# Routing 24 blocks in segments of 6, 6, 4, 4 and 4, and issuing joins and halvings behind copies out of the banks

## The chip, the core and the metric

The kernel runs on one core of one Trainium2 chip. A core has TensorE (PE, with its weight loads shown as PEld), VectorE (DVE), ScalarE (ACT), GpSimd (POOL) and SyncE (SP, which here only issues transfers). Each engine takes its own instructions in the order of the program and waits at one whose inputs or buffers are not ready. Matmul results land in PSUM, in eight banks; ACT and DVE copy them out. The metric is the device time of one execution in microseconds (us), the median of the runs.

## What is computed

A local and global attention, and on its output a mixture of eight experts of which each token takes two.

```python
def _attn_ref(q, k, v, n_global, n_local):      # 4 x 8 heads x 768 x 64; 8 global, 96 local
    ...
    scores = scale * np.matmul(q, k.transpose(0, 1, 3, 2)) + bias
    scores = np.where(keep, scores, -1000000000.0)
    a = np.exp(scores - scores.max(-1))
    return np.matmul(a / (a.sum(-1) + 1e-09), v)

def _moe_ref(x, w_gate, w_noise, noise, w1, w2):  # x 3072 x 512, 8 experts, hidden 1024
    noisy_logits = x @ w_gate + np.log1p(np.exp(x @ w_noise)) * noise
    top2 = np.argpartition(-noisy_logits, 2, axis=1)[:, :2]
    ...                                           # top2_w: softmax over the two
    for e in range(E):
        for k in range(2):
            mask = top2[:, k] == e
            h = np.maximum(x[mask] @ w1[e], 0.0)
            out[mask] += top2_w[mask, k, None] * (h @ w2[e])
```

## The kernel before

The 3072 tokens are 24 blocks of 128. The program writes its order out by hand: the order of calls in the source is the order of instructions on each engine.

**Attention.** A loop goes over half blocks (two of a block's four pairs of heads each). In each it computes scores, the exponential (ACT), transposes, the product with v, and the division (DVE, L910 to L915). Behind a finished block, `gate_t` transposes it (PE L380) and POOL splits its words into 16-bit halves (L236) for a store into `xd`; `gate_l` multiplies it with the gate weights (PE L410) and copies the result out (ACT L413); `gate_s` sums the partial results (PE L423 or L426). Blocks are taken in pairs within a segment: the second of a pair does the matmuls of both. A segment with an odd number of blocks leaves one block alone, which has its own matmuls.

**Routing.** The list `SEG` cuts the blocks into segments. `route(r)` is a generator: each `next` issues a few small instructions, mostly on DVE, that turn the gate results of segment r into the two chosen experts, weights and places. Its own PE work is a running count (L552, L554) and, in groups of up to three blocks, the entry into a table: masks (L579, on POOL for segments up to `CLOSE`, on DVE after), values (L603), six matmuls (L628), one addition (L632). In the attention loop `tick` and `finish` advance the generators of the segments in progress. What is left of the last two is advanced in `slots` between the matmuls of expert 0's first layer (`up(0, f)`, 32 slots of three matmuls). The first 512 tokens of expert 0 come from the segments up to `CLOSE`, so that expert 0 starts when the attention ends; their rows are stored once more, whole, in `xe`. When all segments are routed, `rank` sorts the other seven experts by load and their tokens are gathered.

**Experts.** Every factor is split into a high and a low part (`cut`: ACT rounds, L196; DVE subtracts, L197), and each product is three matmuls. Expert 0 works plainly. Experts 1 to 7 compute their first layer by seven products of half-size blocks (`first`, PE L1426) in four rounds c = 0 to 3; sums and copies out of the banks around them are ACT L1468, L1485, L1491 and L1113, and DVE L1462, L1478, L1500 and L1117. `between(c, slot)` issues what the table `ahead` lists: weights for a later round (`w[c][0..2]`, of which [1] waits for four sums on POOL, L1276 to L1279), halvings of the second layer's weights (`w2_`), gathers (`get`), DMA transposes (`tip`) and joins (`mix`). A join (`weave`, ACT L282 or DVE L284) puts the two 16-bit halves of a gathered, transposed tile together again. The second layer (`second`) is `down` (L1169) and `down_t` (L1192), into a ring of two banks; ACT copies each result of `down_t` out (L1201 for expert 0; L1198 and L1199 for the others), `back` transposes it (L1215), and `put` scales it (L1142) and adds it to the output by an indirect DMA (L1145). While `second(e)` runs, the list that `prepare(e + 1)` returns is worked off beside it: the next expert's tokens, `tokens(e, t)`, in the steps `one` (four sums, L1319 to L1322), `same`, `two` and `three` (halvings, each an ACT L196 and a DVE L197), with weights and joins between. In the traces the names are of the tiles: `aside` holds sums and the copies of `down_t`, `xg` a gathered tile, `xt` its 16-bit form, `wall` weights, `xh` and `xl` the high and the low part of tokens, `hh` and `hl` of the hidden layer.

Of the kernel before, what the change touches and what calls it, by code (L numbers as in the profile page):

```python
# [10 lines left out]
F32 = mybir.dt.float32  # L11
# [10 lines left out]
P = 128  # L22
# [13 lines left out]
def tile_local_global_attention_then_moe(  # L36
# [14 lines left out]
    B, _, _, D, _, HP, Q = q.shape  # L51
    H = 2 * HP
    Dm = H * D
# [3 lines left out]
    E, _, F = w1.shape  # L57
    KC, FC = Dm // P, F // P
    NG = kT.shape[2] // NB - P
    N = B * S  # L60
    NT = B * NB
# [1 line left out]
    windowed = 1 <= n_local <= NP + 1 and 0 <= n_global <= NG  # L63
    scale = 1.0 / math.sqrt(D)
    slopes = [2.0 ** (-8.0 * (h + 1) / H) for h in range(H)]
    SEG = [(0, 6), (6, 12), (12, 17), (17, 21), (21, NT)]
    CLOSE = 2
    SW = max(z - a for a, z in SEG)

# [5 lines left out]
    gp = wctx.enter_context(tc.tile_pool(name="gp", bufs=1))  # L75
# [13 lines left out]
    wd = dram.tile([N, E], F32, name="wd")  # L89
    xe = dram.tile([DUMP + SEG[CLOSE][1] * P, Dm], F32, name="xe")  # L90

# [118 lines left out]
    xg, xt, xw = {}, {}, {}  # L210
# [18 lines left out]
    def planes(x):  # L229
        return x.rearrange("p (h d) -> p h d", h=2)  # L230
# [7 lines left out]
    def gather(e, t, n=DUMP + N):  # L238
        if e >= E or t >= tiles(e):
            return  # L240
        if e == 0 and t < TA:
            n = DUMP + SEG[CLOSE][1] * P
            xw[e, t] = gp.tile([P, Dm], F32, name="xg", bufs=7)
# [115 lines left out]
    XR, XT, LS, stored, rowed = {}, {}, {}, {}, {}  # L359
# [5 lines left out]

    ALONE = [z - 1 for a, z in SEG if (z - a) % 2]

    def partner(g):
        if not windowed or g in ALONE:
            return None  # L370
        a = [a for a, z in SEG if a <= g < z][0]
        return (g - a) % 2

    def gate_t(g):
        x = rowed[g] = XR.pop(g).rearrange("p h d -> p (h d)")
        stored[g] = gp.tile([P, 2 * Dm], U16, name="xt", bufs=4)
        halved(planes(stored[g]), words(x))
        ps = bank("m").rearrange("p (k t) -> p k t", k=KC)
        for k in range(KC):
            nc.tensor.transpose(ps[:, k], x[:, k * P:(k + 1) * P], ident)  # L380
        j = partner(g)
        if j is None:
            XT[g] = ys[2].rearrange("p (k t) -> p k t", k=KC)
            to = XT[g]
        else:
            if j == 0:
                XT[g + 1] = pairs[0].rearrange("p (k j t) -> p k j t", k=KC, j=2)
            to = XT[g + 1 - j][:, :, j]
        nc.scalar.activation(to, ps, AF.Copy)

    def store(g):
# [2 lines left out]
    def gate_l(g, later=None):  # L394
        if g < SEG[CLOSE][1]:
            nc.sync.dma_start(xe[DUMP + g * P:DUMP + (g + 1) * P], rowed.pop(g))
        if later is None:
            store(g)
        else:
            later(store, g)  # L400
        j = partner(g)
        if j == 0:
            return
        ps = bank("m")[:, :P]
        x = XT.pop(g)
        x = [x] if j is None else [x[:, :, i] for i in range(2)]
        for i, y in enumerate(x):
            c = 2 * E * (1 - i)
            for k in range(KC):
                nc.tensor.matmul(ps[32 * k:32 * k + 32], wgn[:, c + 4 * E * k:][:, :4 * E], y[:, k], start=i == 0,  # L410
                                 stop=i + 1 == len(x), tile_position=(0, 32 * k))
        LS[g] = small.tile([P, P], F32, name="ls")
        nc.scalar.activation(LS[g], ps, AF.Copy)  # L413
# [15 lines left out]
    pairs = []  # L429
# [223 lines left out]
    with ExitStack() as actx:  # L653
# [34 lines left out]
        if windowed:  # L688
# [36 lines left out]
            t = small.tile([P, 1], F32, name="warm")  # L725
# [66 lines left out]
        routes, active = {}, []  # L792
# [3 lines left out]

        END, WAIT = 7, 8

        def begin():
            for x, _ in active:  # L800
                x.ready = {WAIT: 4, WAIT + 1: 6}.get(x.ready, 0)

        def go(y):
            x = y[0]
            v = next(x, 0)
            if v == 0:
                active.remove(y)
            elif v is True:
                x.ready = WAIT
            elif v == 2:  # L810
                x.ready = END
            elif v == LAST:
                x.ready = WAIT + 1

        def tick(place):
            for y in sorted(active, key=lambda y: y[1] != CLOSE):
                if y[0].ready <= place:
                    return go(y)

        def finish():  # L820
            for y in active[:]:
                n = 5 if y[1] >= CLOSE else 3
                while n and y in active and y[0].ready <= END:
                    go(y)
                    n -= 1

# [92 lines left out]
        todo = {}  # L919
# [85 lines left out]
        else:  # L1005
# [6 lines left out]
            for g in range(NT):  # L1012
                b, i = divmod(g, NB)
                n = g * HP
# [18 lines left out]
            for n in range(0, NPAIR, 2):  # L1033
                g, odd = divmod(n // 2 - LAG, 2)
# [51 lines left out]
    with ExitStack() as mctx:  # L1086
# [118 lines left out]
        def back(e, i):  # L1205
# [11 lines left out]

        late, last = pending
        slots = {
            0: [(late, 24)], 1: [(gate_s, 2), (late, 27)], 2: [(gate_t, 1), (late, 30)], 3: [(late, 33)],  # L1220
            4: [(gate_l, 1), (late, 36)], 5: [(late, 39)], 6: [(gate_s, 1), (late, 42)], 7: [(late, 45), (last, 2)],
            8: [], 9: [(late, 48), (last, 5)], 10: [(last, 7)], 11: [(last, 8)],
            12: [(late, 52), (last, 9)], 13: [(last, 12)], 14: [(last, 14)], 15: [(late, 54), (last, 16)],
            16: [(last, 19)], 17: [(last, 21)], 18: [(last, 23)], 19: [(last, 26)],
            20: [(last, 30)], 21: [(last, 33)], 22: [(late, 57), (last, 35)], 23: [(last, 37)],
            24: [(last, 39)], 25: [(last, 42)], 26: [(late, 61)], 27: [(last, 45)],
            28: [(last, 48)], 29: [(late, 99), split], 30: [split], 31: [(last, 52)],
        }
        slot, parts = [0], [0]

# [109 lines left out]
        def prepare(e):  # L1340
            get, tip, mix = moves(e)
            if e == 1:
                x, y, z = (tokens(1, t) for t in range(1, 4))
                get = moves(2)[0]
                return [pair[2], join[5], pair[3], x[0], w1_[0], *x[1:3], join[6], x[3], *held[:2], y[0], held[2], *y[1:3],
                        w1_[1], y[3], w1_[2], z[0], *z[1:3], get[0], z[3], get[1]]
            w = [x for c in range(2) for x in weights(e, c)]
            x = [tokens(e, t) for t in range(3 + (tiles(e) > 6))]
            x = [[lambda a=a, b=b: (a(), b()), c, d] for a, b, c, d in x]
            todo = [w[0], *x[0], w[1], *x[1], *x[2]]  # L1350
            if e > 1:
                joins = [lambda j=j: weave(e, fetch[j], nc.vector) for j in range(len(fetch))]
                todo = [w[0], tip[5], *x[0][:2], joins[3], x[0][2], mix[4], w[1], tip[6], *x[1][:2], joins[5], x[1][2]]
                todo += [*x[2][:2], mix[6], x[2][2]]
            if tiles(e) > 6:
                todo += x[3]
            return todo + [w[2]]

        get, tip, mix = moves(1)
        held = []  # L1360
# [3 lines left out]
        for t in range(3):  # L1364
            for i, _ in enumerate(down(0, t, held)):
                for x in early.get((t, i), []):
                    x()
        w0, w1_ = weights(1, 0), weights(1, 1)
        pair = tokens(1, 0)
        join = [lambda j=j: weave(1, fetch[j], (None, nc.vector)[j in (2, 4, 6)]) for j in range(len(fetch))]  # L1370
        ready = {0: [get[5], get[6], w0[0], tip[3]], 1: [join[0], tip[4]], 2: [join[1], tip[5]], 3: [w0[1]],
                 4: [join[2], tip[6]], 5: [join[3], w0[2]], 6: [pair[0]], 7: [pair[1], join[4]]}
        for f in range(FC):
            up(1, f)
            for x in ready[f]:
# [37 lines left out]
        def first(e, before):  # L1413

            h = CAPS[e] // 2
            x = halves(e)
# [13 lines left out]
            w = {c: weights(e, c) for c in (1, 2, 3)}  # L1430

            def w2_(j):
                return lambda: split(e, 2, j)

            get, tip, mix = moves(e + 1)
# [10 lines left out]
            if e == 1:  # L1446
                ahead = {
                    (0, 4): [w2_(0), tip[0]], (0, 5): [w2_(4), get[2]], (0, 6): [w[2][0], tip[1]], (0, 7): [],
                    (1, 4): [w[2][1], get[3]], (1, 5): [mix[0], tip[2]], (1, 6): [w[2][2], w[3][0]],
                    (1, 7): [w2_(1), get[4]],  # L1450
                    (2, 4): [w2_(5), w[3][1], tip[3]], (2, 5): [mix[1]], (2, 6): [w[3][2], get[5]],
                    (2, 7): [w2_(2), mix[2], tip[4]],
                    (3, 4): [w2_(6), get[6]], (3, 5): [w2_(3)], (3, 6): [w2_(7)], (3, 7): [],
                }

            def between(i, slot):
# [72 lines left out]
    left = nc.values_load(more[0:1, E:E + 1], min_val=0, max_val=N)  # L1529
    with tc.If(left > 0), tc.tile_pool(name="lc", bufs=1) as lc:  # L1530
        wov = lc.tile([P, NT, E], F32, name="wov")
        for (a, z), (ixf, sl, we) in zip(SEG, kept):
            w = z - a
# [9 lines left out]
            for j in range(2):  # L1543
                to = eq if j else wov[:, a:z]
# [4 lines left out]
        for e in range(E):  # L1549
            n = nc.values_load(more[0:1, e:e + 1], min_val=0, max_val=N)  # L1550
            with tc.If(n > 0):
# [4 lines left out]
                with tc.For_i(0, NT, 1) as i:  # L1556
                    r = lc.tile([P, E], F32, name="r")
                    x = lc.tile([P, Dm], F32, name="x")
                    xt = lc.tile([P, KC, P], F32, name="xt")
                    ht = lc.tile([P, FC, P], F32, name="ht")  # L1560
                    y = lc.tile([P, Dm], F32, name="y")
# [61 lines left out]
```

## Time and profile before

| What | Value |
|---|---|
| Median of the runs | 700.47 us |
| Lowest | 700.07 us |
| The profiled execution, its own time | 701.94 us |
| Its span, first to last instruction | 700.2 us |
| Mean granted TensorE clock in it | 0.999 |
| PE, PEld busy | 683.6 us (98%), 615.1 us (88%) |
| DVE, ACT, POOL busy | 459.8, 423.6, 324.5 us (66, 60, 46%) |
| DMA, mean over the span | 167 GB/s |

The profiled execution took 1.47 us more than the median, so a difference found in its trace is taken off the median. A matmul's record overlaps the next one's, so that a busy PE can still have lost a little: what shows it is the step from one start to the next.

### The profile page before, as it was taken

Reading aid. Unit: us, or ns where it says so; the run is one execution under the profiler, and the core shown is the slowest. Engines: PE = TensorE matmul, PEld = TensorE weight load, DVE = VectorE, ACT = ScalarE, POOL = GpSimd, SP = SyncE. Lnnn points to the kernel's source line nnn. Section 1 sums busy time; section 2 is a strip of 40 time slices with the busy share of each in tenths; the row PEclk is TensorE's granted clock in tenths of the full one; section 3 lists DMA queues with packets and bytes.
Section 4 is the critical chain, followed back from the end, with each engine's and each line's share of the span. In section 5 each row is a group of like instructions: output and inputs, shape, how many; then the busy total and the mean of one; then the engine's idle time right before and its main releaser. Section 6 shows DMA issues by size and latency. Waiting matters only on the chain. (4 is left out here: it accounts for less than half of the span.)

```text
span 700.2 us, 16023 instructions
## 1 busy us (share of the span) xinstructions
PE 683.6 (98%) x5701; PEld 615.1 (88%) x5701; DVE 459.8 (66%) x1412; ACT 423.6 (60%) x912; POOL 324.5 (46%) x408
## 2 busy tenths in 40 slices
PE   6999999999999999999999999999999999999995
PEld 5888888888889889999999998999899899889984
DVE  7668788968928477656766676667377756757600
ACT  6888787762346576547755755486558647755510
POOL 3352837450288663264536444642645354541222
PEclk9999999999999999999999999999999999999999
DMA  8999978859394877257935884496459457842233
GB/s 249 328 306 313 277 230 282 296 168 359 116 259 91 163 181 158 49 122 136 218 60 122 166 174 75 125 168 148 82 151 249 63 136 163 184 74 91 32 47 49
DMA packets 132889, 116.61 MB, mean 167 GB/s; under 512 B 51866, under 2 KB 97050, under 8 KB 132800
## 3 DMA queue, kind: packets, MB, share of 16 engines
q1 hardware_dynamic: 121392, 89.35, 46.5%
q0 software_dynamic: 11264, 25.89, 20.3%
q8 instruction: 47, 0.77, 0.5%
q14 instruction: 42, 0.34, 0.1%
q10 hardware_dynamic: 144, 0.26, 0.1%
HBM read 71.07 MB, written 33.10 MB: 149 GB/s over the span
## 5 line engine op out<-in xcount | busy, mean ns | idle before, releaser
L1426 PE MATMUL bank<-xh,wall 128*128 128x384 f32 (+4 forms) x784 | 216.9, 342 | 1.0 <-ACT aside L1468 0.6
L1426 PEld LDWEIGHTS bank<-xh,wall 128*128 128x128 f32 x784 | 143.9, 188 | 5.4 <-ACT aside L1468 1.3
L1426 PE MATMUL bank<-xl,wall 128*128 128x384 f32 (+4 forms) x392 | 133.4, 340 | 0.0
L1145 POOL DMA_INDIRECT out_dram<-y,ids x40 | 64.7, 1617 | 124.8 <-ACT y L1142 121.0
L1169 PE MATMUL av<-w2h,hh 128*128 128x512 f32 x304 | 119.8, 394 | 1.5 <-ACT aside L1201 1.1
L197 DVE TENSOR_TENSOR wall<-raw,wall 128x512 fp32r<-128x512 f32 (+1 forms) x84 | 76.5, 918 | 66.3 <-ACT wall L196 66.2
L1169 PE MATMUL av<-w2h,hl 128*128 128x512 f32 x304 | 119.1, 392 | 0.0
L1169 PE MATMUL av<-w2l,hh 128*128 128x512 f32 x304 | 119.1, 392 | 0.0
L196 ACT ACTIVATE wall<-raw 128x512 fp32r<-128x512 f32 (+1 forms) x84 | 58.0, 698 | 47.5 <-POOL raw L1279 47.5
L1117 DVE SCALAR_TENSOR_TENSOR hl<-bank,hh 128x384 fp32r<-128x384 f32 (+4 forms) x84 | 47.1, 561 | 52.8 <-ACT hh L1113 51.8
L1426 PEld LDWEIGHTS bank<-xl,wall 128*128 128x128 f32 x392 | 73.9, 188 | 2.8
L865 ACT ACTIVATE a<-ns,mx 128x168 f32<-128x168 f32 (+1 forms) x192 | 67.8, 422 | 13.5 <-DVE mx L862 13.0
L251 POOL DMA_INDIRECT xg<-xd,ids x49 | 51.9, 1060 | 41.7 <-DVE place L302 29.8
L1169 PEld LDWEIGHTS av<-w2h,hl 128*128 128x128 f32 x304 | 57.1, 188 | 12.6
L862 DVE CUSTOM_DVE_ANT_0 ns<-sc,bias 128x168 f32<-128x168 f32 (+1 forms) x188 | 51.8, 320 | 24.3 <-PE sc L848 8.7
L1169 PEld LDWEIGHTS av<-w2h,hh 128*128 128x128 f32 x304 | 57.1, 188 | 11.0 <-ACT aside L1201 1.3
L1113 ACT ACTIVATE hh<-bank 128x384 fp32r<-128x384 f32 (+4 forms) x84 | 41.9, 498 | 39.2 <-DVE bank L1500 25.5
L1169 PEld LDWEIGHTS av<-w2l,hh 128*128 128x128 f32 x304 | 57.1, 188 | 9.4 <-DVE w2l L197 0.3
L1278 POOL TENSOR_TENSOR raw<-raw 128x256 f32<-128x256 f32 x28 | 22.1, 790 | 77.3 <-DVE wall L197 76.7
L899 PE MATMUL av<-vs,at 128*64 128x65 f32 (+1 forms) x768 | 57.3, 224 | 0.3 <-issue 0.3
L236 POOL COPY xt<-y 128x256 uint16<-128x256 uint16 x96 | 35.0, 401 | 46.7 <-DVE y L915 46.7
L899 PEld LDWEIGHTS av<-vs,at 128*64 128x64 f32 (+1 forms) x768 | 50.8, 136 | 2.4 <-issue 2.0
(219 smaller groups left out, 1465.5 us busy)
## 6 DMA issues: line engine op xcount, KB each, us to landing
raw<-in_w SPq DMA_DIRECT2D x64, 256.0 KB
raw<-in_w SPq DMA_DIRECT2D x32, 512.0 KB
out_dram<-zero SPq DMA_DIRECT2D x14, 512.0 KB
vs<-in_v SPq DMA_DIRECT2D x24, 260.0 KB
xd<-xt SPq DMA_DIRECT2D x24, 256.0 KB
qbuf<-in_q SPq DMA_DIRECT2D x23, 256.0 KB
ks<-in_k SPq DMA_DIRECT2D x20, 272.0 KB
xe<-y SPq DMA_DIRECT2D x17, 256.0 KB
```

The costliest lines, as they stand in the source:

```text
L196: nc.scalar.activation(hi, src, AF.Copy)
L197: eng.tensor_sub(lo, src, hi.bitcast(F32))
L236: nc.gpsimd.tensor_copy(to[:, :, c], frm[:, :, c])
L251: nc.gpsimd.indirect_dma_start(out=xg[e, t].bitcast(U16)[:m], out_offset=None, in_=xd[:n], in_offset=bass.IndirectOffsetOnAxis(ap=r, axis= ...
L862: nc.vector.tensor_tensor_reduce(out=ns[x][:, s, :w], in0=ps[:, s], in1=bias[:, u + x, s] if i else bias0[:, u + x, s], scale=-scale, scal ...
L865: nc.scalar.activation(A[n + x][:, s * w:(s + 1) * w], ns[x][:, s, :w], AF.Exp, bias=mx[x][:, s:s + 1], scale=-1.0)
L899: nc.tensor.matmul(ps[s * Q:(s + 1) * Q, h], a[r:z, part * P + q0:part * P + q0 + Q], t[r:z, c], start=k == 0 and (n == 1 or h == 0), stop ...
L1113: nc.scalar.activation(inner(e)[0][j][:, f, :src.shape[1]], src, AF.Relu)
L1117: nc.vector.scalar_tensor_tensor(lo, src, 0.0, hi.bitcast(F32), op0=OP.max, op1=OP.subtract)
L1145: ins = nc.gpsimd.indirect_dma_start(out=out, out_offset=bass.IndirectOffsetOnAxis(ap=r, axis=0), in_=y, in_offset=None, bounds_check=N + ...
L1169: nc.tensor.matmul(ps, x[j][:, f, cols], w[:, f], start=n == 0, stop=n == 3 * FC - 1)
L1426: nc.tensor.matmul(ps, wb[c % 2][u][:, 2 * a + k], x[v][:, 2 * b + k], start=start and n == 0, stop=stop and n == 5, skip_group_check=True)
```

## The change

`SEG` gets segments of 6, 6, 4, 4 and 4 blocks for 6, 6, 5, 4 and 3. No block stands alone any more, and the last pair, 22 and 23, is kept in two tiles of the `xg` ring, since the pair's own tile is given up with the attention. `PACE` limits a segment's steps in the attention to six a half block for segments 3 and 4; as the counter is set at the start of a half block, a segment that starts within one, with no other in progress, waits for the next. The slots of `up(0)` are set anew. In `prepare` and in `ahead`, joins and halvings get other places.

```diff
-    SEG = [(0, 6), (6, 12), (12, 17), (17, 21), (21, NT)]
+    SEG = [(0, 6), (6, 12), (12, 16), (16, 20), (20, NT)]
...
-            if j == 0:
-                XT[g + 1] = pairs[0].rearrange("p (k j t) -> p k j t", k=KC, j=2)
-            to = XT[g + 1 - j][:, :, j]
+            if j == 0 and g == NT - 2:
+                XT[g + 1] = [gp.tile([P, Dm], F32, name="xg", bufs=7).rearrange("p (k t) -> p k t", k=KC) for _ in "ab"]
+            elif j == 0:
+                x = pairs[0].rearrange("p (k j t) -> p k j t", k=KC, j=2)
+                XT[g + 1] = [x[:, :, i] for i in range(2)]
+            to = XT[g + 1 - j][j]
...
+        PACE = (99,99,99,6,6)
+        left = [0]
+
         def begin():
+            left[0] = max([PACE[r] for _, r in active], default=0)
...
-                if y[0].ready <= place:
+                if y[0].ready <= place and left[0] > 0:
...
-            0: [(late, 24)], 1: [(gate_s, 2), (late, 27)], 2: [(gate_t, 1), (late, 30)], 3: [(late, 33)],
+            0: [(late, 33)], 1: [(late, 35)], 2: [(gate_t, 1), (late, 37)], 3: [(late, 39)],
...
-                return [pair[2], join[5], pair[3], x[0], w1_[0], *x[1:3], join[6], x[3], *held[:2], y[0], held[2], *y[1:3],
-                        w1_[1], y[3], w1_[2], z[0], *z[1:3], get[0], z[3], get[1]]
+                return [*pair[2:], x[0], *join[4:6], w1_[0], *x[1:3], join[6], x[3], *held[:2], y[0], held[2], *y[1:3],
+                        *w1_[1:], y[3], *z[:3], *get[:2], z[3]]
...
-                todo = [w[0], tip[5], *x[0][:2], joins[3], x[0][2], mix[4], w[1], tip[6], *x[1][:2], joins[5], x[1][2]]
+                todo = [w[0], tip[5], *x[0][:2], joins[3], x[0][2], w[1], tip[6], *x[1][:2], mix[4], joins[5], x[1][2]]
...
-                 4: [join[2], tip[6]], 5: [join[3], w0[2]], 6: [pair[0]], 7: [pair[1], join[4]]}
+                 4: [join[2], tip[6]], 5: [join[3], w0[2]], 6: [pair[0]], 7: [pair[1]]}
...
-                    (1, 4): [w[2][1], get[3]], (1, 5): [mix[0], tip[2]], (1, 6): [w[2][2], w[3][0]],
-                    (1, 7): [w2_(1), get[4]],
+                    (1, 4): [w2_(1), get[3]], (1, 5): [mix[0], tip[2]], (1, 6): [get[4]],
+                    (1, 7): [w[2][1], w[2][2]],
```

Three places of the order on ACT, each before and with the change. The first is the second layer of expert 0, where expert 1's tokens are made ready. L196 is a halving, L282 a join, L1201 (L1209 with the change) a copy of `down_t` out of its bank.

```order
L1113 ACTIVATE hh<-sc 128x300
L196 ACTIVATE xh<-xg 128x4x128
L196 ACTIVATE xh<-xg 128x2x128
L282 ACTIVATE xg<-xt 128x2x512
L196 ACTIVATE xh<-aside 128x8x128
L1201 ACTIVATE aside<-av 128x300
L196 ACTIVATE wall<-raw 128x512
```

```order
L1121 ACTIVATE hh<-sc 128x300
L196 ACTIVATE xh<-xg 128x4x128
L196 ACTIVATE xh<-xg 128x2x128
L196 ACTIVATE xh<-aside 128x8x128
L1209 ACTIVATE aside<-av 128x300
L282 ACTIVATE xg<-xt 128x2x512
L196 ACTIVATE wall<-raw 128x512
```

The join moved from ahead of the halving of the sums and of the first copy to behind both. On DVE the join that stood ahead of the low parts of the same tokens moved behind them in the same way. Further down the same queue the third copy moved ahead of a halving of sums (`xh<-aside`) that it stood behind.

The second place is the first layer of expert 1, rounds 1 and 2: L1491 (L1499) and L1468 (L1476) are copies out of the banks, `wall` weights of the first layer, `w2h` of the second.

```order
L1113 ACTIVATE hh<-bank 128x406
L196 ACTIVATE wall<-raw 128x768
L1491 ACTIVATE aside<-bank 128x406
L282 ACTIVATE xg<-xt 128x2x512
L1113 ACTIVATE hh<-bank 128x406
L196 ACTIVATE wall<-raw 128x512 x2
L196 ACTIVATE w2h<-raw 128x512
L1468 ACTIVATE aside<-bank 128x406
```

```order
L1121 ACTIVATE hh<-bank 128x406
L196 ACTIVATE w2h<-raw 128x512
L1499 ACTIVATE aside<-bank 128x406
L282 ACTIVATE xg<-xt 128x2x512
L1121 ACTIVATE hh<-bank 128x406
L196 ACTIVATE wall<-raw 128x768
L196 ACTIVATE wall<-raw 128x512
L1476 ACTIVATE aside<-bank 128x406
```

The weights that wait for POOL went from ahead of the copy L1491 to just ahead of L1468, one halving of the second layer took their place, and one piece of the next round's weights left this stretch.

The third place is the second layer of expert 3, where expert 4's tokens are made ready; the other experts from 2 on have the same rows in other sizes. L1198 and L1199 (L1206 and L1207) are the copies of `down_t`.

```order
L196 ACTIVATE xh<-aside 128x8x128
L1198 ACTIVATE aside<-av 128x256
L1199 ACTIVATE aside<-av 128x24
L282 ACTIVATE xg<-xt 128x2x512
L196 ACTIVATE wall<-raw 128x768
L196 ACTIVATE xh<-xg 128x4x128
L1198 ACTIVATE aside<-av 128x256
L1199 ACTIVATE aside<-av 128x24
L196 ACTIVATE xh<-xg 128x2x128
```

```order
L1206 ACTIVATE aside<-av 128x256
L1207 ACTIVATE aside<-av 128x24
L196 ACTIVATE wall<-raw 128x768
L196 ACTIVATE xh<-xg 128x4x128
L196 ACTIVATE xh<-xg 128x2x128
L1206 ACTIVATE aside<-av 128x256
L1207 ACTIVATE aside<-av 128x24
L282 ACTIVATE xg<-xt 128x2x512
L196 ACTIVATE xh<-aside 128x8x128
```

The join moved behind the weights, two halvings and the next copy out of a bank.

## Rows read from the trace of the kernel before

**Rows 1.** Windows by stage: length, busy time (instructions) of each engine, PEclk, DMA share, GB/s.

```profile
155.70:183.00 27.30, 27.30 (x147) 22.04 (x144) 23.31 (x108) 9.50 (x21) 0.74 (x2) 1.00 0.79 289
213.00:231.10 18.10, 16.75 (x112) 15.80 (x111) 16.27 (x28) 11.28 (x23) 15.48 (x13) 1.00 0.38 70
231.10:270.00 38.90, 37.86 (x199) 35.50 (x198) 25.00 (x44) 26.82 (x51) 22.13 (x21) 1.00 0.85 188
...
sum 700.20, PE 683.59 PEld 615.05 DVE 459.83 ACT 423.55 POOL 324.49; mean PE 97.66 PEld 87.86 DVE 65.69 ACT 60.51 POOL 46.36
```

**Rows 2.** Waits of PE: for what, us in total, times, longest us.

```profile
PE av L1169 <- ACT aside L1201: 1.1, 1, 1.1
PE bank L1426 <- ACT aside L1468: 0.6, 2, 0.3
PE bank L1215 <- ACT aside L1198: 0.6, 1, 0.6
...
PE bank L1426 <- DVE aside L1462: 0.4, 1, 0.4
PE av L1169 <- ACT aside L1199: 0.4, 1, 0.4
...
PE av L1192 <- ACT aside L1201: 0.3, 1, 0.3
PE lg L628 <- POOL xt L236: 0.2, 1, 0.2
```

**Rows 3.** Timeline of PE at the attention's end: start, us, operation, count of records.

```profile
155.09 0.64 PE L410 MATMUL m<-pair,wgn 128*32 128x128 f32 x16
...
160.20 0.43 PE L410 MATMUL m<-y,wgn 128*32 128x128 f32 x8
```

**Rows 4.** Windows of two half blocks of the attention with the same PE work, as rows 1.

```profile
104.03:106.65 2.62, 2.62 (x58) 2.32 (x55) 2.41 (x16) 2.16 (x7) 1.40 (x2) 1.00 0.04 10
122.70:125.60 2.90, 2.90 (x59) 2.52 (x55) 2.90 (x30) 2.17 (x6) 0.75 (x2) 1.00 1.06 378
```

**Rows 5.** Timeline of DVE in expert 0's first layer.

```profile
160.38 0.69 DVE L1117 SCALAR_TENSOR_TENSOR hl<-at,hh 128x512 fp32r<-128x512 f32 x1 [0.69 <-ACT hh L1113]
...
161.65 0.48 DVE L579 TENSOR_SCALAR wall<-iota_p,aside 128x128 fp32r<-128x128 f32 x2
162.04 0.50 DVE L603 TENSOR_TENSOR xg<-aside 128x336 fp32r<-128x336 f32 x1
```

**Rows 6.** Timeline of ACT in expert 0's second layer; in brackets the idle time before.

```profile
219.87 0.42 ACT L1201 ACTIVATE aside<-av 128x300 f32<-128x300 f32 x1 [2.48 <-DVE xl L197]
...
226.85 1.06 ACT L196 ACTIVATE xh<-aside 128x1024 fp32r<-128x1024 f32 x1 [2.34 <-DVE aside L1322]
```

**Rows 7.** Timeline of DVE in the same stretch.

```profile
215.95 1.31 DVE L284 COPY xg<-xt 128x1024 uint16<-128x1024 uint16 x1
...
218.02 1.75 DVE L197 TENSOR_TENSOR xl<-aside,xh 128x1024 fp32r<-128x1024 f32 x1
220.84 0.69 DVE L197 TENSOR_TENSOR wall<-raw,wall 128x512 fp32r<-128x512 f32 x1 [1.07 <-ACT wall L196]
...
230.92 0.35 DVE L197 TENSOR_TENSOR xl<-xg,xh 128x88 fp32r<-128x88 f32 x2
```

**Rows 8.** Timeline of PE where expert 1's first product begins.

```profile
231.14 0.34 PE L1426 MATMUL bank<-xh,wall 128*128 128x406 f32 x1
...
231.32 0.35 PE L1426 MATMUL bank<-xl,wall 128*128 128x406 f32 x1
```

**Rows 9.** Timeline of ACT in expert 1's first layer, rounds 1 and 2.

```profile
248.64 0.85 ACT L196 ACTIVATE wall<-raw 128x768 fp32r<-128x768 f32 x1 [2.28 <-POOL raw L1279]
...
252.95 0.51 ACT L1468 ACTIVATE aside<-bank 128x406 f32<-128x406 f32 x1
```

**Rows 10.** Timeline of ACT in expert 3's second layer.

```profile
415.42 1.39 ACT L282 ACTIVATE xg<-xt 128x1024 uint16<-128x1024 uint16 x1 [2.54 <-DMA xt<-xg]
```

**Rows 11.** Timeline of DVE, a join of the same size later.

```profile
420.92 0.76 DVE L284 COPY xg<-xt 128x1024 uint16<-128x1024 uint16 x1
```

More of the change, by code (lines that the diff above doesn't have):

```diff
@@ L405, in gate_l @@
         x = XT.pop(g)
-        x = [x] if j is None else [x[:, :, i] for i in range(2)]
+        x = [x] if j is None else x
         for i, y in enumerate(x):
@@ L804, in go @@
             x = y[0]
+            left[0] -= 1
             v = next(x, 0)
@@ L822, in finish @@
                 n = 5 if y[1] >= CLOSE else 3
-                while n and y in active and y[0].ready <= END:
+                while n and y in active and y[0].ready <= END and left[0] > 0:
                     go(y)
@@ L1219, in tile_local_global_attention_then_moe @@
         slots = {
-            0: [(late, 24)], 1: [(gate_s, 2), (late, 27)], 2: [(gate_t, 1), (late, 30)], 3: [(late, 33)],
[L1221 to L1227, printed above, removed]
+            0: [(late, 33)], 1: [(late, 35)], 2: [(gate_t, 1), (late, 37)], 3: [(late, 39)],
+            4: [(gate_l, 1), (late, 42)], 5: [(late, 45)], 6: [(gate_s, 1), (late, 48)], 7: [(last, 2)],
+            8: [(late, 52), (last, 5)], 9: [(last, 8)], 10: [(late, 54), (last, 10)], 11: [(last, 13)],
+            12: [(late, 57), (last, 15)], 13: [(last, 18)], 14: [(last, 21)], 15: [(late, 61), (last, 23)],
+            16: [(last, 26)], 17: [(late, 99)], 18: [(last, 30)], 19: [(last, 33)],
+            20: [(last, 36)], 21: [(last, 39)], 22: [(last, 42)], 23: [(last, 45)],
+            24: [(last, 48)], 25: [], 26: [(last, 52)], 27: [(last, 54)],
+            28: [(last, 57)], 29: [split], 30: [(last, 61), split], 31: [(last, 63)],
         }
@@ L1448, in first @@
                     (0, 4): [w2_(0), tip[0]], (0, 5): [w2_(4), get[2]], (0, 6): [w[2][0], tip[1]], (0, 7): [],
-                    (1, 4): [w[2][1], get[3]], (1, 5): [mix[0], tip[2]], (1, 6): [w[2][2], w[3][0]],
-                    (1, 7): [w2_(1), get[4]],
-                    (2, 4): [w2_(5), w[3][1], tip[3]], (2, 5): [mix[1]], (2, 6): [w[3][2], get[5]],
-                    (2, 7): [w2_(2), mix[2], tip[4]],
-                    (3, 4): [w2_(6), get[6]], (3, 5): [w2_(3)], (3, 6): [w2_(7)], (3, 7): [],
+                    (1, 4): [w2_(1), get[3]], (1, 5): [mix[0], tip[2]], (1, 6): [get[4]],
+                    (1, 7): [w[2][1], w[2][2]],
+                    (2, 4): [w[3][0], w2_(5), tip[3]], (2, 5): [mix[1]], (2, 6): [w[3][1], get[5]],
+                    (2, 7): [w[3][2]],
+                    (3, 4): [w2_(2), mix[2], tip[4], get[6]], (3, 5): [w2_(6)], (3, 6): [w2_(3)], (3, 7): [w2_(7)],
                 }
```

## The prediction

> **What bounds the kernel now.** I read the windows by stage first, then the waits of PE, then timelines at the waits that the change touches. The windows show PE busy 683.59 of the 700.20 us span, 97.66%, at a granted clock of 1.00 in each stage shown, the upper of its two levels [rows 1]. So the time is PE's work plus its gaps, and only two things help: less work for PE, or a shorter gap. DVE, ACT and POOL have slack on average (459.83, 423.55 and 324.49 us), but not everywhere: in expert 0's second layer (213 to 231.1 us) DVE works 16.27 of 18.1 us, and there PE loses 1.35 us [rows 1]. The list of PE's waits says what the gaps end on. Most of those behind expert 0 end on a copy out of a bank that came late (L1201, L1468, L1198, L1199, and L1462 on DVE) [rows 2]. They are short, and with PE's wait for L628 they add up to 3.6 us of 700. With the overlap of the next paragraph that is the ceiling of what reordering can give.
>
> The idle column understates each a little. A matmul of 406 columns is recorded with 0.34 to 0.35 us, while the next one starts 0.18 us later (231.14, then 231.32) [rows 8]: the records overlap by 0.16 us. At a stop that overlap is lost too, so a stop costs about 0.16 us more than its idle time.
>
> **The change, part by part.** The sum is made against the profiled 701.94 us (span 700.20 plus 1.74 around it), which is 1.47 above the median; the difference is then taken off the median.
>
> **A, the attention.** In the trace of before a block that stands alone costs 0.43 us of gate matmuls, a pair 0.64 [rows 3]. Two lone blocks (16 and 23) become one pair more: 2 x 0.43 - 0.64 = 0.22 us less for PE. The table's matmuls are two a block, so their number stays. PE's one wait for L628 (0.2 us idle, 0.36 with the lost overlap) came from the masks of a segment behind a halving L236 on POOL [rows 2]; those masks now have most of a half block more, and I take 0.3 us off. Against this stands what DVE does to the half blocks. Two of them with the same PE work last 2.62 and 2.90 us: the longer one has 30 instructions on DVE for 16, and DVE is full in it (2.90 of 2.90) [rows 4]. So a burst of routing costs 0.28 us. The change moves bursts: segment 2 is shorter and starts earlier, segment 3 takes its paced steps inside the attention. The number of steps there hardly changes, so I take nothing for the bursts, with four half blocks more or fewer as bounds: 4 x 0.28 = 1.1 either way. A is -0.5, between -1.6 and +0.6; if the wait for L628 stays as well, up to +0.9. The store of one block to `xe` that goes was on SP with DMA nearly idle there (10 GB/s in one of these windows [rows 4]); I count nothing for it.
>
> **B, expert 0's first layer.** PE is never idle in it (27.30 of 27.30) while DVE works 23.31 [rows 1]. The last segment has one block more to enter into the table: two masks 0.48 and the values 0.50, so 1.0 us more for DVE [rows 5], against some nine steps of segment 3 that the slots no longer hold. With 4.0 us of slack that fits. What is tight is the first group of six table matmuls. It now stands ten slots in (a slot is 27.30 / 32 = 0.85 us), so PE comes to it at about 164.2; DVE starts three masks and values after the attention's last work, in the trace of before from 161.65 at 1.0 us each with one L1117 of 0.69 between [rows 5], which by the same pace, with the routing's steps ahead of them gone, ends near 164.0. The new two tiles of `xg` for the last pair add a wait for a ring buffer in front of ACT's copy of the transposed gate input, and behind it in ACT's queue stand the copies of the first products. No row shows that wait; it lies inside the bounds. I take +0.1, between 0 and +1.0 (one block's masks and values late).
>
> **C, expert 1's tokens.** In the second layer of expert 0 ACT's copy L1201 starts at 219.87 after waiting 2.48 us for DVE: it writes to `aside`, where DVE still reads sums until 218.02 + 1.75 = 219.77, behind its own join [rows 6, 7]. Later a halving of sums at 226.85 waits 2.34 for DVE's L1322, with the third copy behind it [rows 6]. PE waits 0.3 and 1.1 us for these two copies [rows 2], with overlap 0.46 and 1.26, so 1.7. In the new order DVE reads those sums ahead of its join, 1.3 us earlier, and the third copy stands ahead of the sums' halving; both stops go. But PE does not keep it all. DVE's chain of low parts, from the join at 215.95 to the last at 230.92 + 0.35 [rows 7], idles only 1.07 us (at 220.84, for a halving that ACT had behind the same copy), and PE's first matmul with a low part starts at 231.32, just as that chain ends [rows 8]. A PE that comes 1.7 us earlier meets DVE there. So the gain is what DVE's chain shortens: at most the 1.07 us, at least nothing. Joins queued later delay what they make ready (the third and fourth tile of tokens), which stands at the chain's end and not in its middle. I take the middle, -0.6.
>
> One row gives a reason for the low end. DVE's join takes 1.31 us at 215.95, with POOL busy 15.48 of 18.1 us in that stage, and the same join 0.76 us at 420.92 [rows 1, 7, 11]. The Trainium skill (SBUF — State Buffer, "Who interferes with whom") says that DVE and GpSimd share a port pair as an exclusive lock, so that the second waits in full. The longer join agrees with it. By it the chain's length would be set by POOL's work, which the change leaves whole, C would be 0 and the sum 0.6 us less.
>
> **D, expert 1's first layer.** ACT stands 2.28 us for weights that POOL has to sum (L1279) and only then halves them and copies (248.64, then L1468 at 252.95) [rows 9]. PE pays 0.6 in two stops for L1468 and 0.4 for DVE's L1462 [rows 2]: 1.0, and with three overlaps 1.5. In the new order a halving that waits for nothing takes the weights' place, and they come a step later, when POOL is done. The last round's second piece, `w[3][1]`, now also has less time ahead of its use. I take -1.3: at best -1.5, at worst -0.3, if the wait for POOL shows up one copy further on. Here PE gains for good, since nothing in the next stage is due at a fixed time.
>
> **E, experts 2 to 7.** In expert 3's second layer a join on ACT waits 2.54 us for a DMA transpose [rows 10], in front of the copies for which PE then waits 0.6 and 0.4 us [rows 2]; with two overlaps 1.3. Now weights, two halvings and the next copy stand ahead of the join, so that ACT comes to it only behind PE's next result; what is left of the 2.54 us holds up the halving of sums behind it, and no copy. I take -1.2, between -1.25 and -0.6 (one of the two comes back as a wait for that halving). In the other experts the same row moves, but their copies show no wait worth a row, so nothing goes and nothing comes; the cover is the tokens' lead of a whole layer.
>
> Sum: -0.5 + 0.1 - 0.6 - 1.3 - 1.2 = -3.5 us, so 698.4 for the profiled execution and **697.0 us** for the median (0.5%).
>
> **The rivals.** First: the stops move on and half the gain is given back. POOL's sums in D and DVE's chain in C are the true limits, and a reordered queue only meets them at another instruction. Then C is 0, A's removed wait is eaten by a burst (0), D is half (-0.65), E stays: 0 + 0.1 + 0 - 0.65 - 1.2 = -1.75, so 698.7. For it: 2.28 us of ACT waiting for POOL [rows 9], and DVE 90% busy in C [rows 1]. Against: the copies themselves depend on neither.
>
> Second, on the other side: DVE falls behind in expert 0's first layer. The last segment now ends in its last slot, and all that follows hangs on its last addition: the ranking, the gathers, the transposes, the joins and DVE's chain, which has no slack at its end (231.27 against PE's 231.32 [rows 7, 8]). So each microsecond by which the addition is late is paid in full at expert 1's first product. The other terms without C give -2.9; with the chain late by 2.9 us the kernel is back at its time, and above that it is slower: 5 us late gives 702.6. For it: one block more in that segment. Against: DVE's 4.0 us of slack [rows 1], and only 1.0 more work [rows 5].
>
> Third: the bursts of routing mostly vanish from the attention, since the paced steps fill half blocks with room; then A is at its bound, -1.6, and the time 695.9.
>
> Fourth: the change doesn't do what it says. The copies move ahead in the queue, but each waits by itself, as the first L1201 does for DVE's reading of `aside` [rows 6]; no stop goes, and only the 0.22 us of gate matmuls remain: 700.2.
>
> **How the numbers follow.** The forecast, with A to E near their values (some 696 to 698.2), has 0.52; the first rival 0.24, the second 0.10 (most of it just above 700.5), the third 0.08, the fourth 0.06. The bounds of the terms sum to -1.6 + 0 - 1.1 - 1.5 - 1.25 = -5.45 below and 0.9 + 1.0 + 0 - 0.3 - 0.6 = +1.0 above, that is 695.0 to 701.5, and the runs of before spread by 0.4 (700.07 to 700.47). The lower bounds all at once, with that spread, give 694.6; above I stop at 701.2, since all upper bounds at once are the less likely and only half of the second rival lies beyond. A measurement of this kernel tells about 2%, 14.0 us, from no change. No case but the second rival at its far end (DVE more than 17 us late) reaches 714.5, and none reaches 686.5: faster 0.01, within 2% 0.97, slower 0.02 (cases not thought of lie in the ends).
>
> **What the changed profile would show.** PE's waits for L1201, L1468 and L1198 (eight lines further down there) gone or under 0.2 us, the wait for the weights on ACT in expert 1 short, the attention's end within 1 us of 155.7 less 0.5, and PE never idle in expert 0's first layer. C is right if PE reaches expert 1's first low part 0.6 to 1.1 us earlier relative to the attention's end, and idles there for a DVE at work. What would make the prediction wrong: the ranking later than now by more than 2 us, bursts in more half blocks, or ring buffers that the later joins hold longer, so that gathers start late and a DMA transpose ends a wait of PE.

## The result, and the profile after

The change makes the kernel slower: 705.45 us median against 700.27 of the kernel before in the same session, a ratio of 1.006 (95% interval 1.0045 to 1.0075). This ratio and those below leave out runs far above the rest (one of the kernel before took 835.5 us); they are not the quotients of the medians beside them, which come out equal or up to 0.0014 higher. The profiled execution took 705.55 us (span 703.8), 3.6 us more than the profiled one of before. The forecast was 697.0, and the range, up to 701.2, does not hold the time.

The traces are cut where the work of PE changes: at the first product of expert 0's first layer, of its second layer, and of experts 1, 2, 3 and 4. First the kernel before in windows at these cuts (length; busy time of PE, PEld, DVE, ACT, POOL with instructions; granted clock as a share of 2.4 GHz; DMA share; GB/s):

```profile
0.00:155.66 155.66, 149.75 (x2830) 128.96 (x2830) 119.42 (x741) 123.71 (x347) 75.32 (x172) 1.00 0.86 274
155.66:181.14 25.48, 25.48 (x139) 20.71 (x136) 21.49 (x106) 7.64 (x17) 0.74 (x2) 1.00 0.84 310
181.14:231.14 50.00, 48.38 (x290) 43.69 (x290) 34.14 (x78) 24.93 (x46) 36.81 (x42) 1.00 0.66 145
231.14:293.85 62.71, 61.67 (x345) 57.65 (x344) 41.70 (x78) 39.79 (x79) 27.36 (x25) 1.00 0.64 137
293.85:361.53 67.68, 67.68 (x375) 63.22 (x374) 44.95 (x78) 41.41 (x81) 31.96 (x30) 1.00 0.68 133
361.53:429.40 67.87, 66.93 (x376) 61.88 (x374) 45.14 (x78) 41.02 (x81) 32.75 (x31) 1.00 0.66 135
429.40:700.20 270.80, 263.69 (x1363) 238.95 (x1361) 152.98 (x258) 145.04 (x266) 119.55 (x109) 1.00 0.57 119
```

The changed kernel in the same windows:

```profile
0.00:160.86 160.86, 149.65 (x2824) 128.55 (x2825) 119.19 (x752) 123.62 (x348) 75.89 (x174) 1.00 0.84 263
160.86:188.48 27.62, 26.39 (x144) 20.85 (x142) 21.80 (x93) 6.64 (x14) 0.81 (x2) 1.00 0.77 285
188.48:236.79 48.31, 47.88 (x290) 43.53 (x288) 33.04 (x72) 25.97 (x46) 35.43 (x41) 1.00 0.66 147
236.79:298.84 62.05, 61.01 (x345) 57.82 (x344) 42.45 (x83) 39.99 (x78) 28.11 (x26) 1.00 0.77 143
298.84:366.42 67.58, 67.58 (x375) 63.14 (x374) 45.18 (x78) 41.59 (x81) 33.50 (x30) 1.00 0.67 136
366.42:432.76 66.34, 66.34 (x375) 61.84 (x374) 45.07 (x78) 41.03 (x81) 32.77 (x30) 1.00 0.65 135
432.76:703.80 271.04, 263.70 (x1363) 238.91 (x1361) 153.25 (x258) 144.84 (x266) 119.10 (x108) 0.99 0.59 118
```

By lengths: attention +5.20, expert 0's first layer +2.14, then -1.69, -0.66, -0.10, -1.53 and +0.24, in sum +3.60. PE's busy time in the attention is the same (149.65 for 149.75); its idle time grew from 5.91 to 11.21, so the loss there is waiting. In the layer behind it 1.23 of the 2.14 us are idle time. The rest is PE's busy time, 26.39 for 25.48: a pair's gate matmuls for one block's [rows 3], 16 table matmuls for 14, and the overlaps lost at the stops. The two stages lose 7.3 us together; the four behind them gain 4.0 and the last loses 0.2 in these two executions.

The waits of PE after (what, total us, times, longest) name the places; they answer to [rows 2]:

```profile
...
PE lg L426 <- ACT aside L416: 1.5, 1, 1.5
PE sc L856 <- issue: 1.3, 1, 1.3
PE sc L856 <- DVE aside L493: 1.1, 1, 1.1
PE bank L1434 <- DVE xl L197: 1.0, 1, 1.0
PE sc L856 <- PE m L380: 0.9, 1, 0.9
PE lg L555 <- DVE tab L635: 0.8, 1, 0.8
PE m L413 <- ACT pair L392: 0.8, 2, 0.4
PE av L1177 <- DVE w2l L197: 0.3, 1, 0.3
PE lg L631 <- DVE aside L499: 0.3, 1, 0.3
...
```

None of the waits of [rows 2] for L1201, L1468, L1462, L1198 and L1199 is left. In their place stand waits of the scores (L856) for routing steps on DVE (L493), and one at expert 1's first low part (L1434). Two rows name no engine that could have held PE ("issue", and PE's own L380). There PE started its next scores at 123.37 and 132.18, each time just after DVE had begun to read the scores before, which stood behind routing steps (the first of them at 122.58, below).

The collision is best seen on DVE, from half block 37 on (start, us, operation; idle time before in brackets):

```profile
115.48 0.42 DVE L923 TENSOR_TENSOR y<-av,den 128x256 f32<-128x256 f32 x1 [1.35 <-POOL wall L582]
...
116.16 0.57 DVE L606 TENSOR_TENSOR xg<-aside 128x336 fp32r<-128x336 f32 x1
...
117.08 0.87 DVE L491 SCALAR_TENSOR_TENSOR aside<-aside 128x32 f32<-128x32 f32 x3
117.88 0.32 DVE L870 CUSTOM_DVE_ANT_0 ns<-sc,bias 128x168 f32<-128x168 f32 x1
...
118.48 0.18 DVE L493 SCALAR_TENSOR_TENSOR aside<-aside 128x32 f32<-128x32 f32 x1
...
120.33 1.31 DVE L606 TENSOR_TENSOR xg<-aside 128x336 fp32r<-128x336 f32 x2
...
122.58 0.33 DVE L870 CUSTOM_DVE_ANT_0 ns<-sc,bias 128x168 f32<-128x168 f32 x1
```

L606 is segment 1's entry into the table (second group), L491 and L493 are segment 2's first steps. In the kernel before segment 1 was alone here: DVE went from L915 through three values to the scores. Now two segments' steps lie ahead of the scores (L870) in one queue, behind a wait for POOL of 1.35 us; that wait is in the kernel before too, with 0.93 us. The scores come at 117.88 and 122.58, and PE waits for them.

### The profile page after: what moved, and what is told of

Read it like the earlier page. It is cut to its first block, busy times and chain, and to the rows that moved or that the text cites. A ratio compares the mean times of both kernels' runs of the same rounds, so it can differ in the third digit from the quotient of the medians.

```text
span 703.8 us, 16008 instructions
## 1 busy us (share of the span) xinstructions
PE 682.5 (97%) x5699; PEld 614.7 (87%) x5699; DVE 460.0 (65%) x1411; ACT 423.7 (60%) x911; POOL 325.6 (46%) x410
## 4 chain that ended last, share of the span: by engine, by line
PE 82%; issue 6%; DVE 6%; POOL 3%; ACT 2%; DMA 1%; POOLq 0%; DVEq 0%; ACTq 0%
PE bank L1434 28%; PE av L1177 22%; PE av L1200 7%; PE av L907 6%; PE at L886 5%; PE sc L856 4%; PE at L1140 2%; PE sc L1140 2%; POOL out_dram L1153 1%; PE m L380 1%; DVE xl L197 1%; POOL xt L236 1%; PE m L413 1%; PE bank L1223 1%; PE lg L631 1%
## 5 line engine op out<-in xcount | busy, mean ns | idle before, releaser
L1434 PE MATMUL bank<-xh,wall 128*128 128x384 f32 (+4 forms) x784 | 215.9, 342 | 0.0
L1434 PEld LDWEIGHTS bank<-xh,wall 128*128 128x128 f32 x784 | 144.0, 188 | 3.3
L1434 PE MATMUL bank<-xl,wall 128*128 128x384 f32 (+4 forms) x392 | 133.4, 340 | 1.0 <-DVE xl L197 1.0
L196 ACT ACTIVATE wall<-raw 128x512 fp32r<-128x512 f32 (+1 forms) x84 | 58.0, 700 | 45.5 <-POOL raw L1287 45.5
L1434 PEld LDWEIGHTS bank<-xl,wall 128*128 128x128 f32 x392 | 73.9, 188 | 3.9 <-DVE xl L197 1.4
L870 DVE CUSTOM_DVE_ANT_0 ns<-sc,bias 128x168 f32<-128x168 f32 (+1 forms) x188 | 52.1, 321 | 23.9 <-PE sc L856 9.2
```

What stands on the lines that cost most here:

```text
L196: nc.scalar.activation(hi, src, AF.Copy)
L870: nc.vector.tensor_tensor_reduce(out=ns[x][:, s, :w], in0=ps[:, s], in1=bias[:, u + x, s] if i else bias0[:, u + x, s], scale=-scale, scal ...
L1434: nc.tensor.matmul(ps, wb[c % 2][u][:, 2 * a + k], x[v][:, 2 * b + k], start=start and n == 0, stop=stop and n == 5, skip_group_check=True)
```

## The experiments

Theory 1: the four-block segment 2 starts two half blocks earlier, while segment 1 still enters its blocks, and with precedence over it; both segments' steps then stand ahead of the scores on DVE. Theory 2: the new wait for the next half block shifts segments 0 and 1 to worse places. Theory 3: the new order of joins and halvings gains only where PE comes late, and little by itself.

**The order alone (e1), the segments alone (e2).** e1 is the kernel before with the new `prepare` and `ahead`; e2 is the changed kernel with the old ones. The first lines of e1's edit, which e2 makes the other way round:

```diff
-                return [pair[2], join[5], pair[3], x[0], w1_[0], *x[1:3], join[6], x[3], *held[:2], y[0], held[2], *y[1:3],
+                return [*pair[2:], x[0], *join[4:6], w1_[0], *x[1:3], join[6], x[3], *held[:2], y[0], held[2], *y[1:3],
...
```

> The kernel before with only the new places of joins and halvings; segments, pace and slots as before. In the trace of the changed kernel the attention is 5.2 us longer and expert 0's first layer 2.1, the stages behind them 4.0 us shorter in sum. Theory 1 (the segments cost it, the new order gains 4.0 by itself): 696.3 us, between 695.5 and 697.2; PE's waits for L1201, L1468 and L1198 are gone. Rival (the new order gains only because a later PE finds its inputs ready; without the delay the stops move on): 698.5 to 700.3.

> The changed kernel with the places of joins and halvings as before; segments, pace and slots are the new ones. Theory 1 (both parts add up): 705.45 + 4.0 = 709.4 us, between 708.4 and 710.4. Rival (the stops that the order removes were already covered by the longer attention): 705.5 to 707.5.

e1 took 699.26 us against 700.96 of before in that session: 0.9971 (0.9959 to 0.9984), by the ratio 2.0 us less, and e2 709.06: 1.0106 (1.0077 to 1.0135), 7.4 us more. The signs are theory 1's, and the two ratios add up to 1.0077; the distance to the change's 1.006 lies within e2's interval. e2's time is in theory 1's range, e1's in its rival's. By the ratios, on the 700.27 us from which the forecasts were made, both lie between the two (698.2 and 707.7). In size the order gives half of the 4.0 us that the two traces showed. Theory 3 falls only in part: the order gains without PE's delay, but less than forecast. The waits of PE in e1:

```profile
PE sc L848 <- DMA ks<-in_k: 4.9, 1, 4.9
PE bank L1426 <- DVE xl L197: 1.5, 1, 1.5
PE av L899 <- issue: 0.3, 1, 0.3
PE lg L628 <- ACT aside L472: 0.3, 1, 0.3
```

All stops that the order was to remove are gone, and 1.5 us of the gain is waited off at expert 1's first low part. So the rival is right for that part: a stop moved on. Most of what the trace of before overstated seems to be expert 3, as far as one other execution can show: its stops of 1.0 us hung on a join that waited 2.54 us for a transfer [rows 10]. In e2, which has the old order there, the same join on ACT waited half as long:

```profile
423.19 1.38 ACT L282 ACTIVATE xg<-xt 128x1024 uint16<-128x1024 uint16 x1 [1.28 <-DMA xt<-xg]
```

Expert 3's stage, from its first product to expert 4's, is 66.61 us in e2 and 66.34 in the changed kernel (0.3 less), and was 67.87 in the profiled execution of before.

**No wait for the next half block (e3).**

```diff
-            left[0] = max([PACE[r] for _, r in active], default=0)
+            left[0] = max([PACE[r] for _, r in active], default=99)
```

> The changed kernel in which a segment that starts within a half block, with none in progress, goes on at once, as before, instead of waiting for the next half block. Segment 0's table entries then fall one half block earlier. Theory 2 (that wait pushes the entries into half blocks with gate matmuls, 0.7 us in half blocks 22 to 27): 704.7 us. Theory 1 (the loss sits in half blocks 36 to 43 and in expert 0's first layer): 705.4, no difference to the changed kernel beyond 0.7.

705.31 us, 1.0059 (1.0038 to 1.0079), no difference to the change's 1.006. The 0.7 us that theory 2 forecast lie within this interval, so the runs alone don't refute them. The traces show less: from the gate matmuls of half block 22 to those of half block 30 it is 24.79 us in e3, 24.96 in the changed kernel and 24.77 in the kernel before. Theory 2 is worth 0.2 us there, of an attention that is 5.2 longer.

**Segment 2 two half blocks later (e4).**

```diff
-                            active.append((Steps(route(ends.index(g))), ends.index(g)))
+                            start = lambda r=ends.index(g): active.append((Steps(route(r)), r))
+                            if ends.index(g) == CLOSE:
+                                at(n + 2, start)
+                            else:
+                                start()
```

> The changed kernel with the start of segment 2 (blocks 12 to 15) put off by two half blocks, to half block 37, where it started before with five blocks. Theory 1 (its steps, which have precedence, collide on DVE with segment 1's last table entries in half blocks 35 to 38): PE's stalls of 1.4, 0.3, 1.3 and 0.9 us there go, 701.5 to 703 us. Rival (the work of routing has to go somewhere: later it meets the gathers for expert 0 and segment 3): 705 to 707.

701.34 us, 1.0005 (0.9992 to 1.0018): 3.9 us less than the change by the ratios, at the lower end of theory 1's forecast and far from the rival's. Half blocks 37 and 38, first in the kernel before, then in the changed kernel, then in e4:

```profile
116.90:120.16 3.26, 3.07 (x48) 2.58 (x45) 2.86 (x23) 3.03 (x12) 1.68 (x5) 1.00 0.84 220
120.16:122.70 2.54, 2.54 (x45) 2.06 (x44) 2.40 (x14) 2.06 (x7) 0.74 (x2) 1.00 0.98 337
```

```profile
116.94:120.75 3.81, 2.46 (x40) 1.67 (x37) 3.71 (x25) 2.04 (x6) 1.46 (x5) 1.00 0.98 309
120.75:127.14 6.39, 4.64 (x74) 3.58 (x70) 5.39 (x38) 3.63 (x11) 0.54 (x1) 1.00 0.98 337
```

```profile
117.18:120.70 3.52, 3.21 (x47) 2.42 (x44) 3.12 (x22) 2.92 (x11) 2.18 (x6) 1.00 1.02 342
120.70:123.81 3.11, 3.11 (x61) 2.44 (x59) 2.97 (x19) 1.89 (x5) 0.75 (x2) 1.00 1.03 367
```

In half block 38 PE idles 1.75 us beside 38 instructions on DVE, in e4 not at all beside 19. (The table matmuls of segment 1 stand in 37 in e4, in 38 in the change.) Over half blocks 37 to 40 PE idles 4.05 us in the changed kernel and 0.31 in e4. The attention ends at 156.92 instead of 160.86. The total work of routing is the same; its place is what costs. Not all of the 3.9 us is this collision: a wait of 1.5 us in half block 43, behind L416, goes too, and waits elsewhere come (more on it below).

**The older segment first (e7).**

```diff
-            for y in sorted(active, key=lambda y: y[1] != CLOSE):
+            for y in sorted(active, key=lambda y: y[1]):
```

> The changed kernel with one key changed: in the attention the older segment's steps go first, where segment 2 had precedence over segment 1. Segment 2 still starts in half block 35. Theory 1 in the form that the precedence makes the collision (two segments' steps ahead of the scores): 702 to 703.5 us, half blocks 37 to 40 shorter by 2 to 3 us in sum. Rival (the early start as such, the total of steps in those half blocks, costs it): 704.5 to 706.

701.99 us, 1.0023 (1.001 to 1.0037): 2.6 us less than the change, with segment 2 still starting as early. The rival falls. But the half blocks did not shorten as expected. Half block 40 of the changed kernel, then 37, 38 and 40 of e7:

```profile
130.00:135.50 5.50, 4.55 (x70) 3.92 (x67) 4.84 (x26) 3.64 (x11) 5.50 (x10) 1.00 0.76 234
```

```profile
116.89:123.53 6.64, 4.75 (x46) 3.68 (x44) 4.05 (x24) 2.04 (x6) 2.61 (x6) 0.74 1.02 343
123.53:128.65 5.12, 3.85 (x65) 2.79 (x64) 4.82 (x42) 3.00 (x9) 0.00 (x0) 1.00 0.58 206
131.34:135.49 4.15, 4.15 (x71) 3.84 (x67) 4.15 (x21) 2.75 (x8) 4.15 (x8) 1.00 1.01 306
```

38 and 40 gain (5.12 for 6.39, 4.15 for 5.50 us), but 37 takes 6.64 us for 3.81. PE waits there 1.9 us for DVE's L491, does the table matmuls that stood in 38, and runs in part at the lower clock (0.74 in this window). By the start of half block 41 the two traces are level (135.49 and 135.50). The 1.86 us by which e7's attention ends earlier (159.00 for 160.86) lie behind that place, where PE no longer waits for L416. The lower clock took about 1.7 us in half block 37 (an estimate: 0.26 of 6.64), and this execution lies 1.45 us above e7's median; at the full clock the four half blocks would be shorter by about as much. So the precedence costs 2.6 us by the runs, but how much of that is the collision, and how much the wait for L416, is not shown.

**The table's addition ahead of the last segment's steps (e5).**

```diff
-            12: [(late, 57), (last, 15)], 13: [(last, 18)], 14: [(last, 21)], 15: [(late, 61), (last, 23)],
-            16: [(last, 26)], 17: [(late, 99)], 18: [(last, 30)], 19: [(last, 33)],
+            12: [(late, 57), (last, 15)], 13: [(last, 18)], 14: [(last, 21)], 15: [(late, 61)],
+            16: [(late, 99), (last, 23)], 17: [(last, 26)], 18: [(last, 30)], 19: [(last, 33)],
```

> The changed kernel with segment 2 put off by two half blocks (as in e4), and in expert 0's first layer segment 3's last table addition issued one slot earlier, ahead of the steps 22 to 26 of the last segment. Theory 1 (PE's stop of 1.2 us at the last segment's running count is DVE's order: the addition stands behind twelve small steps of the last segment): the stop goes, and as ranking and all behind it follow, 701.3 - 1.0 = 700.3 us. Rival (DVE is short of time there, the stop only moves to the next table matmuls): 701.3, with the waits for L631 longer by about 1 us.

699.97 us against 699.75, 0.9999 (0.9985 to 1.0013). Against e4 the ratio fell by 0.4 us, less than either interval, so the runs don't settle it. The trace shows the stop shrink and change its reason, from L635 to the last segment's own step:

```profile
172.28 0.18 PE L555 MATMUL lg<-aside,upper 128*128 128x32 bf16 x1 [0.30 <-DVE aside L523]
```

Expert 0's first layer is 27.09 us in it, for 27.62 in e4 and 25.48 before: half of the 1.0 us came. What stays there are waits (0.3 us at L555; 0.3 and 0.2 at L631), a pair's gate matmuls for one block's (0.21 [rows 3]) and the two table matmuls more. In the attention of e5 PE still waits 1.9 us in two stops for a pair's copy L392 on ACT; the longer, 1.5, comes in half block 46, where segment 3's paced steps lie ahead of the scores. Even so its attention ends at 155.77 us, as in the kernel before (155.66), and 1.15 us earlier than in e4, whose attention has the same code: by so much two executions can differ there. Against e1 (0.9971) that leaves the segments 2.0 us to the bad.

**The weights ahead of the join (e6).** e1 with one more step moved:

```diff
-                return [*pair[2:], x[0], *join[4:6], w1_[0], *x[1:3], join[6], x[3], ...
+                return [*pair[2:], x[0], join[4], w1_[0], join[5], *x[1:3], join[6], x[3], ...
```

> The kernel before with only the new order of joins and halvings (as in e1), and in expert 0's second layer ACT halves the weights ahead of its join instead of behind it. DVE stands 1.07 us for that halving in e1's trace. Theory 1 (DVE's chain of low parts sets when expert 1's first product goes on, so that what PE gained upstream is waited off there): the 1.5 us of waiting of PE at expert 1's first low part shrinks to 0.5, 699.3 - 1.0 = 698.2 us. Rival (something else, as POOL's work beside it, sets that chain's length): 699.3, the idle time comes back elsewhere on DVE.

697.23 us against 699.75: 0.9962 (0.9946 to 0.9978), the fastest of all kernels here, by the ratio 2.7 us below the one before and faster than the changed one. Against e1 (0.9971) the difference lies within the intervals. PE's wait at the first low part was 1.4 us in its trace, not 0.5. But the profiled execution took 699.54 us, 2.3 above e6's median; eight of the twelve took 696.9 to 697.5. Ahead of the step that was moved, ACT's join at 213.01 waits 3.02 us for a transfer in this trace, in e1 0.97. The same subtraction on DVE, in e1 and in e6:

```profile
220.30 0.69 DVE L197 TENSOR_TENSOR wall<-raw,wall 128x512 fp32r<-128x512 f32 x1 [1.07 <-ACT wall L196]
```

```profile
220.77 1.22 DVE L197 TENSOR_TENSOR wall<-raw,wall 128x512 fp32r<-128x512 f32 x1
...
222.47 1.83 DVE L197 TENSOR_TENSOR xl<-xg,xh 128x512 fp32r<-128x512 f32 x2 [0.49 <-ACT xh L196]
```

The 1.07 us of waiting are gone, but 0.53 come back in the operation itself and 0.49 in a wait for the next halving. In e1 POOL stood still beside it (from 219.8 to 221.1), in e6 it was at a sum (L1277, from 220.32 for 1.11 us). So POOL's work beside DVE has a share in the chain's length, as the rival says. From the low part of the sums to its end the chain is still 0.44 us shorter than in e1 (14.17 for 14.61). Whether PE's wait shrinks in e6's usual execution, as theory 1 has it, is not shown. By the ratio e6 is at 698.3 us in e1's session, near theory 1's 698.2, but not clear of e1.

## Why the prediction was wrong

**A failed**, and with it the forecast. The step is "so I take nothing for the bursts, with four half blocks more or fewer as bounds: 4 x 0.28 = 1.1 either way". The attention became 5.2 us longer. The price of 0.28 us came from one burst of a single segment, 30 instructions for 16, on a DVE that was just full [rows 4]. It does not hold for two segments in the same half blocks: there DVE has 3.71 and 5.39 us of work (half blocks 37 and 38) beside 2.46 and 4.64 on PE, the scores come late behind the steps of two segments, PE waits for them, and the next half block begins late. I had written that segment 2 "starts earlier", and had counted steps in the whole attention instead of DVE's work ahead of the scores in half blocks 36 to 40. e4 shows the early start to be the cause: 3.9 us of the loss go with a later start alone, and PE's idle time in half blocks 37 to 40 falls from 4.05 to 0.31. PE's wait of 1.5 us for L416 in half block 43 goes with them, and its cause stays open (below). The lone blocks' 0.22 us and the wait for L628 are too small to be seen beside it.

**B was too small**: 2.14 us for "+0.1, between 0 and +1.0". The first group of table matmuls came without a wait, as worked out; the stops came later, at the last segment's running count (0.8 us idle, 1.0 with the overlap) and at L631. The slot was a little too long, too: the layer's 32 slots last 25.48 us, the 27.30 of [rows 1] reach into the next stage. I had also counted no PE time for the work that moves in here, and 0.9 us of the 2.14 is busy time. I had compared sums (DVE's slack of 4.0 us against 1.0 us more work), while at the running count the order in DVE's queue decided. e5 moved one addition and took back 0.5 us of PE's time in the trace.

**C was right in its mechanism.** PE came 1.69 us earlier through expert 0's second layer and then waited 1.2 with the overlap, so 0.5 are left for 0.6 forecast; in e1 1.85 less 1.66, 0.2. The wait is for DVE's chain, as said. **D** gave 0.66 + 1.2 = 1.86 us in the trace of after, for 1.3, beyond the bound of 1.5: all three stops went. **E** gave 1.53 us against that one trace, but by e2 0.3 in an execution where the transfer lands earlier. Of the order's terms this one was mis-sized: a stop behind a transfer was taken from a single execution that lay 1.47 us above the median. The order's whole gain by the runs is 2.0 us (1.1 to 2.9), for 3.1 forecast.

Of the rivals the second, slower, came nearest: DVE falls behind. But its mechanism was another. It was to be a late last addition, paid at expert 1's first product; instead PE stopped in the attention itself. The first rival's C of 0 lies nearer to e1's 0.2, the forecast's 0.6 nearer to the changed kernel's 0.5. The Trainium skill (SBUF — State Buffer, "Who interferes with whom") says that a DVE instruction with two inputs in SBUF contends with a GpSimd instruction that reads SBUF. e6's 1.22 us for 0.69 beside POOL's sum agrees with that.

One thing stays open: PE's wait of 1.5 us for L416, the copy of a gate result, in half block 43. ACT started that copy at 143.84, after 2.64 us of waiting, though its matmuls are recorded from 141.25 for 0.65 us. It lies among POOL's gathers for expert 0, is in e2 and e3 too (1.4 each), and not in e4, e5 and e7, where segment 2's routing runs later. In the three traces that have it the copy starts 0.5 to 0.6 us behind the end of the fourth gather. It does not belong to the early start as such, since e7 starts as early. What held the copy was not tried.

## What to carry to other kernels

Where small work shares a queue with work that a full engine waits for, count what stands ahead of it in each iteration: one burst cost 0.28 us here, and keeping two from meeting in the same iterations took 3.9 us off, with no step added or removed. A stop that ends on a transfer should be sized from more than one execution before it enters a sum. Two changes delivered together deserve to be run apart: here one half gave 2.0 us and the other cost 7.4.

## What was not expected of the hardware

Behind a stall TensorE's clock fell in some executions and not in others. In e2 PE stood behind the same collision as in the changed kernel, idle for 1.74 of the 7.52 us of half block 38, and then ran at 1.2 GHz for about 6.8 us (0.18 x 7.52 and 0.45 x 4.52, over the half that is lost). Half blocks 38 and 39 of e2, with the granted clock as the third figure from the end:

```profile
120.57:128.09 7.52, 5.78 (x74) 4.48 (x70) 5.38 (x38) 4.13 (x12) 0.53 (x1) 0.82 0.87 281
128.09:132.61 4.52, 4.52 (x64) 3.90 (x61) 1.68 (x11) 1.20 (x3) 2.46 (x5) 0.55 0.92 288
```

The second, half block 39, took 2.86 us at full clock in the changed kernel (127.14 to 130.00) and 4.52 here, with PE busy throughout. The attention of e2 ends at 163.49, for 160.86 with the same code. In e7 the clock fell too, in half block 37 (0.74 in its window); in these half blocks it did not fall in the profiled executions of the changed kernel and of e4. So a part of e2's 7.4 us may be the clock: three of its four executions have a mean of 0.993 or 0.994, those of the changed kernel 0.995 to 0.998.
